# Block-sparse attention with a routed expert layer on one core: the chunk bounds computed with the queries as the stationary operand

## The chip, the cores and the metric

The kernel runs on one core of one Trainium2 chip. The metric is the device time of one execution in microseconds (us). A core has TensorE (PE, matrix products; it reads on-chip memory and writes only into PSUM, its result memory), VectorE (DVE) and ScalarE (ACT), which work on elements and read PSUM, GpSimd (POOL), and SyncE (SP), which here starts transfers. The engines run beside each other and wait for each other through semaphores.

A matrix product on PE has a stationary operand, which a weight load (PEld in the profile) puts into the array, and a moving operand, which is streamed through it; the result has one row per stationary column and one column per moving column. A turn is a transposition on PE: a product with the identity. In this kernel the scores and masks are bf16; keys, queries, bounds and values are fp32 on PE.

## The reference

Four batches, eight heads, 768 positions, head dimension 64. Keys come in 24 chunks of 32. For each query and chunk an upper bound of the scores is computed from the smallest and the largest key entries of the chunk; the six best chunks that are not in the future are kept, and attention runs on them alone. The heads' outputs then go through an expert layer with one of eight experts per token.

```python
k_min = np.min(k_chunks, axis=3)
k_max = np.max(k_chunks, axis=3)
ub = np.sum(np.maximum(q[:, :, :, None, :] * k_min[:, :, None, :, :],
                       q[:, :, :, None, :] * k_max[:, :, None, :, :]), axis=-1)
causal = pos[:, None] // chunk >= np.arange(nc)[None, :]
ub = np.where(causal, ub, -1000000000.0)
top_chunks = np.argsort(ub, axis=-1)[..., -top_k:]
scores = scale * np.matmul(q, k.transpose(0, 1, 3, 2))
# only keys of the chosen chunks, and not of the future; softmax; times v
...
expert_idx = np.argmax(x @ w_gate, axis=1)     # then relu(xe @ w1[e]) @ w2[e], times the gate
```

Since max(q a, q b) = (q (a + b) + |q| |a - b|) / 2, the bound is, up to a factor that does not matter for the order, a sum of two matrix products: q with (k_max + k_min), and |q| with (k_max - k_min).

## The kernel before

The 32 heads are worked on in 16 pairs; the two heads of a pair lie on partitions 0 to 63 and 64 to 127. Work is laid out in a fixed order on each engine: while pair `i` is in attention, the bounds and the selection of pair `n = i + 1` and the turns of keys and queries of pair `m = i + 2` are slipped in between. The order of the lines below is the order on each engine.

The first 128 queries have at most four chunks to see, so they need no selection. The bounds of the other 640 are computed with the chunk sums `ksd` stationary (2 heads x 32 columns) and 320 queries moving, twice for each half, the halves in different partitions of the result. So the bounds come out with chunks on partitions; ACT copies them to on-chip memory (`ub_a`), and three turns (`sel_mm`) bring the queries onto partitions, where DVE can rank along a row.

```python
c0s = (0, 128, 192)
...
        def ub():
            pu = ps_m.tile([128, 384], FP32, tag="m", name="pu")
            for w_, nm in ((0, "qT"), (1, "qA")):
                x_ = s[nm][:].rearrange("p a c -> p (a c)")
                for h in range(2):
                    nc.tensor.matmul(pu[64 * h:64 * h + 64, 0:320], lhsT=ksd[:, w_].rearrange("p a c -> p (a c)"),
                                     rhs=x_[:, ds(128 + 320 * h, 320)],
                                     start=(nm == "qT"), stop=(nm == "qA"), skip_group_check=True)
            s["pu"] = pu

        def ub_a():
            s["ubT"] = work.tile([128, 384], FP32, tag="ud", name="ubT")
            nc.scalar.activation(s["ubT"][:, 0:320], s["pu"][:, 0:320], AF.Copy)

        def sel_mm():
            pt = ps_m.tile([128, 3, 2, 2, 32], FP32, tag="m", name="pt")
            for t in range(3):
                nc.tensor.transpose(pt[:, t], s["ubT"][:, ds(c0s[t], 128)], ident_f[:])
            s["pt"] = pt

        def sel_v():
            ...                      # ubm = pt + cbias, 288 columns
            for t in range(3):
                for hf in range(2):
                    for hd in range(2):
                        nc.vector.max(out=top8[:, t, hf, hd], in_=ubm[:, t, hf, hd])
            ...                      # nsel = ubm < sixth best, 288 columns

        def mask():                  # six turns of nsel into pm
            ...
        def mask_a():                # ACT copies pm into qsb
            ...
```

One round of the loop, cut to what stands around these steps (groups 0 to 2 of four):

```python
                elif g == 0:
                    ...
                    av(i, 0)
                    av(i, 1)
                    ...
                    add(i, 1)
                    run(prep, n, "ub")
                    run(prep, n, "ub_a")
                    ...
                elif g == 1:
                    for u in (4, 5):
                        scores(i, u)
                        exps(i, u)
                    run(prep, n, "sel_mm")
                    if i > 0:
                        run(prep, m, "k_mm", 0)      # turns of the next but one keys
                        run(prep, m, "k_a", 0)
                    if router:
                        rank_mm()
                    run(prep, n, "sel_v")
                    ...
                    av(i, 2)
                    av(i, 3)
                    add(i, 3)
                    ...
                    scores(i, 6, True)
                    exps(i, 6)
                    ...
                elif g == 2:
                    ...
                    run(prep, n, "mask")
                    run(prep, n, "mask_a")
                    ...
                    av(i, 4)
                    av(i, 5)
```

`scores` writes into one of two PSUM buffers, `exps` is the exponential on ACT that frees it, `av` the product with the values, `add` the row sums on DVE. PSUM tiles of the tag "m" share three buffers in turn. The first pair has its own opening, in which `spin(n)` issues n products of ones, so that PE does not stand still.

Of the kernel before, what the change touches and what calls it, by code (L numbers as in the profile page):

```python
# [10 lines left out]
FP32 = mybir.dt.float32  # L11
BF16 = mybir.dt.bfloat16
# [12 lines left out]
def kernel(  # L25
# [10 lines left out]
    nc = tc.nc  # L36
# [22 lines left out]
    c0s = (0, 128, 192)  # L59
# [16 lines left out]
    cbias = const.tile([128, 3, 2, NCH], FP32)  # L76
# [18 lines left out]
    KSD = [buf.tile([128, 2, 2, 32], FP32, name=f"KSD{i}") for i in range(2)]  # L95
    bm = buf.tile([128, 2, NCH], BF16, name="bm")
    nsel = buf.tile([128, 3, 2, 2, 32], BF16, name="nsel")
# [5 lines left out]
    def consts_first():  # L103
# [18 lines left out]
        for t in range(3):  # L122
            nc.gpsimd.affine_select(out=cbias[:, t], in_=cbias[:, t], pattern=[[320, 2], [-CH, NCH]],
                                    compare_op=ALU.is_ge, fill=NEG, base=128 + c0s[t], channel_multiplier=1)
# [57 lines left out]
    def prep_steps(i):  # L182
# [23 lines left out]
        def kse():  # L206
            kt2 = work.tile([128, 2, NCH], FP32, tag="top8", name="kt2")
            nc.vector.tensor_tensor(kt2[:, 0], s["kmx"][:], s["kmn"][:], ALU.add)
            nc.vector.tensor_tensor(kt2[:, 1], s["kmx"][:], s["kmn"][:], ALU.subtract)
            nc.vector.tensor_tensor(ksd[:, :, :, 0:NCH], kt2[:].unsqueeze(2).to_broadcast([128, 2, 2, NCH]),  # L210
                                    bm[:].unsqueeze(1).to_broadcast([128, 2, 2, NCH]), ALU.mult)
# [21 lines left out]
        def ub():  # L233
            pu = ps_m.tile([128, 384], FP32, tag="m", name="pu")
            for w_, nm in ((0, "qT"), (1, "qA")):
                x_ = s[nm][:].rearrange("p a c -> p (a c)")
                for h in range(2):
                    nc.tensor.matmul(pu[64 * h:64 * h + 64, 0:320], lhsT=ksd[:, w_].rearrange("p a c -> p (a c)"),
                                     rhs=x_[:, ds(128 + 320 * h, 320)],
                                     start=(nm == "qT"), stop=(nm == "qA"), skip_group_check=True)  # L240
            s["pu"] = pu

        def ub_a():
            s["ubT"] = work.tile([128, 384], FP32, tag="ud", name="ubT")
            nc.scalar.activation(s["ubT"][:, 0:320], s["pu"][:, 0:320], AF.Copy)

        def sel_mm():
            pt = ps_m.tile([128, 3, 2, 2, 32], FP32, tag="m", name="pt")
            for t in range(3):
                nc.tensor.transpose(pt[:, t], s["ubT"][:, ds(c0s[t], 128)], ident_f[:])  # L250
            s["pt"] = pt

        def sel_v():
            pt = s["pt"]
            ubm = work.tile([128, 3, 2, 2, NCH], FP32, tag="ubm")
            nc.vector.tensor_tensor(ubm[:].rearrange("p n h d c -> p (n h) d c"),
                                    pt[:].rearrange("p n h d c -> p (n h) d c")[:, :, :, 0:NCH],
                                    cbias[:].rearrange("p n h c -> p (n h) c").unsqueeze(2)
                                    .to_broadcast([128, 6, 2, NCH]), ALU.add)
            top8 = work.tile([128, 3, 2, 2, 8], FP32, tag="top8")  # L260
            for t in range(3):
                for hf in range(2):
                    for hd in range(2):
                        nc.vector.max(out=top8[:, t, hf, hd], in_=ubm[:, t, hf, hd])
            u3 = ubm[:].rearrange("p a b c n -> p (a b c) n")
            t3 = top8[:].rearrange("p a b c n -> p (a b c) n")
            nc.vector.tensor_tensor(nsel[:].rearrange("p a b c n -> p (a b c) n")[:, :, 0:NCH], u3,
                                    t3[:, :, TOPK - 1:TOPK].to_broadcast([128, 12, NCH]), ALU.is_lt)

        def mask():  # L270
            pt = ps_m.tile([64, S], BF16, tag="m", name="pm")
            for hf in range(2):
                for t in range(3):
                    nc.tensor.transpose(pt[:, ds(128 + 320 * hf + c0s[t], 128)],  # L274
                                        nsel[:, t, hf].rearrange("p a n -> p (a n)"), ident_b[:])
            s["pm"] = pt

        def mask_a():
            for hd in range(2):
                nc.scalar.activation(qsb[64:64 + NCH, hd, 128:S], s["pm"][32 * hd:32 * hd + NCH, 128:S], AF.Copy)  # L280

        return dict(ub_a=ub_a, mask_a=mask_a, k_mm=k_mm, k_v=k_v, k_a=k_a, kse=kse, q_mm=q_mm, q_v=q_v, q_a=q_a, ub=ub,
                    sel_mm=sel_mm, sel_v=sel_v, mask=mask)


# [397 lines left out]
    def first_pair():  # L683
# [45 lines left out]
        consts_route(colf)  # L729
        prep[0]["ub"]()  # L730
        prep[0]["ub_a"]()
        kt(1)
        spin(8)
        prep[0]["sel_mm"]()
        spin(20)
        ubm = work.tile([128, 3, 2, 2, NCH], FP32, tag="ubm")
        top8 = work.tile([128, 3, 2, 2, 8], FP32, tag="top8")
# [3 lines left out]

        def select(hf):
            nc.vector.tensor_tensor(ubm[:, :, hf], s["pt"][:, :, hf, :, 0:NCH],
                                    cbias[:, :, hf].unsqueeze(2).to_broadcast([128, 3, 2, NCH]), ALU.add)
            for t in range(3):
                for hd in range(2):
                    nc.vector.max(out=top8[:, t, hf, hd], in_=ubm[:, t, hf, hd])
# [295 lines left out]
```

The softmax here doesn't subtract the row's maximum and nothing guards it: scores larger than these inputs give would overflow.

## Time and profile before

| What | Value |
|---|---|
| Time, median of three runs | 351.94 us (351.68 to 352.61) |
| Span of the profiled execution | 355.5 us |
| Mean granted TensorE clock | 0.988 of full |
| PE busy in 60 to 90 us | 29.79 of 30 us |
| DVE busy in 60 to 90 us | 27.95 of 30 us |
| ACT busy in 60 to 90 us | 25.32 of 30 us |
| Bounds on PE (L238), loads and products | 64 + 64 each for q and for its size |
| Copy of the bounds on ACT (L245) | 16 times, 446 ns (median) |
| Turns of the bounds on PE (L250) | 48 times, 273 ns (median) |
| Addition of the causal term on DVE (L256) | 15 times, 451 ns (median) |
| Maxima on DVE (L264) | 180 times, 168 ns (median) |
| Comparison on DVE (L267) | 15 times, 462 ns (median) |
| Turns of the mask on PE (L274) | 90 times, 219 ns (median) |

How to read it: the page of the profile gives first the busy time of each engine and its share of the span, then the span in 40 slices, each digit the busy share of that slice in tenths. Matmuls overlap[...]; so the distance from one start to the next says what a matmul costs, and its length does not. A weight load is listed apart (PEld) and usually runs beside the matmul before it. The rows below the first come from one profiled execution, the first from runs without a profile.

### The profile page before, as it was taken

Reading aid. Unit: us, or ns where it says so; the run is one execution under the profiler, and the core shown is the slowest. Engines: PE = TensorE matmul, PEld = TensorE weight load, DVE = VectorE, ACT = ScalarE, POOL = GpSimd, SP = SyncE. Lnnn points to the kernel's source line nnn. Section 1 sums busy time; section 2 is a strip of 40 time slices with the busy share of each in tenths; the row PEclk is TensorE's granted clock in tenths of the full one; section 3 lists DMA queues with packets and bytes.
Section 4 is the critical chain, followed back from the end, with each engine's and each line's share of the span. In section 5 each row is a group of like instructions: output and inputs, shape, how many; then the busy total and the mean of one; then the engine's idle time right before and its main releaser. Section 6 shows DMA issues by size and latency. Waiting matters only on the chain. (4 is left out here: it accounts for less than half of the span.)

```text
span 355.5 us, 7585 instructions
## 1 busy us (share of the span) xinstructions
PE 329.2 (93%) x2382; PEld 177.2 (50%) x2392; DVE 229.5 (65%) x776; ACT 230.4 (65%) x373; POOL 186.7 (53%) x300
## 2 busy tenths in 40 slices
PE   7889999999999999999999999977995899999992
PEld 7545656556555555555565555534441344444440
DVE  6688999999999999999999999941730000000000
ACT  2588788788796887886887977613323454544551
POOL 8515434536475437284355477583574556655323
PEclk9999999999999999999999999989998999999999
DMA  9998998899585897765979954969694999998962
GB/s 175 205 209 152 167 184 169 153 190 167 104 211 113 161 178 155 152 171 114 186 137 181 182 122 113 209 124 197 137 227 121 227 185 216 194 231 160 216 154 80
DMA packets 132071, 59.83 MB, mean 168 GB/s; under 512 B 122811, under 2 KB 122813, under 8 KB 132032
## 3 DMA queue, kind: packets, MB, share of 16 engines
q1 hardware_dynamic: 120640, 29.91, 43.5%
q0 software_dynamic: 11392, 29.42, 40.0%
q8 instruction: 21, 0.34, 0.4%
q14 instruction: 18, 0.15, 0.1%
HBM read 56.14 MB, written 10.51 MB: 188 GB/s over the span
## 5 line engine op out<-in xcount | busy, mean ns | idle before, releaser
L339 DVE TENSOR_TENSOR Pa<-Pa,Pr 128x768 f32<-128x768 f32 (+2 forms) x109 | 80.5, 742 | 4.3
L318 POOL TENSOR_SCALAR_AFFINE_SELECT Pr<-Pr 128x256 f32<-128x256 f32 x78 | 36.9, 492 | 77.9 <-ACT Pr L314 77.9
L314 ACT ACTIVATE Pr<-ps 128x768 f32<-128x768 f32 x79 | 62.6, 819 | 10.7 <-ACT KTE L203 4.3
L653 PE MATMUL py<-w_all,hT 128*128 x220 | 52.4, 379 | 3.0 <-issue 1.7
L298 PE MATMUL ps<-QSB,KTE 128*128 128x384 bf16 (+4 forms) x352 | 50.4, 283 | 1.5 <-ACT Pr L314 0.2
L661 POOL DMA_INDIRECT out_dram<-y,ti_all x28 | 28.0, 1001 | 37.2 <-ACT y L660 32.1
L298 PEld LDWEIGHTS <-KTE 128*128 128x128 bf16 (+1 forms) x352 | 26.5, 102 | 28.4 <-issue 22.0
L641 PE MATMUL ph<-w_all,KTE 128*128 x116 | 31.1, 413 | 6.3 <-ACT h__3986 L644 3.6
L653 PEld LDWEIGHTS <-hT 128*128 128x128 bf16 x224 | 21.8, 98 | 29.5 <-issue 1.8
L314 ACT ACTIVATE Pa<-ps 128x768 f32<-128x768 f32 x32 | 26.0, 812 | 14.0 <-PE ps L298 12.6
L660 ACT ACTIVATE y<-py,gt_all 128x512 f32<-128x512 f32 x27 | 18.6, 687 | 25.0 <-PE py L653 19.4
L203 ACT ACTIVATE KTE<-pk 64x384 bf16<-64x384 f32 x60 | 29.3, 488 | 7.1 <-DVE kmn L198 6.7
L493 POOL DMA_INDIRECT xs_dram<-xrow,sli x24 | 25.6, 1065 | 7.8 <-issue 5.7
L641 PE MATMUL ph<-w_all,QSB 128*128 x94 | 22.6, 379 | 1.6 <-DMA QSB<-xgqT 1.5
L641 PEld LDWEIGHTS <-KTE 128*128 128x128 bf16 x120 | 12.3, 104 | 23.0 <-issue 9.6
L280 ACT ACTIVATE QSB<-pm 24x640 bf16<-24x640 bf16 x30 | 20.8, 692 | 2.8 <-PE pm L274 2.1
L614 DVE TENSOR_TENSOR ti_all<-xgqA,inv_i 128x1 int32<-128x1 int32 x9 | 1.4, 160 | 30.7 <-DMA xgqA<-xs_dram,grow 26.1
L157 POOL DMA_DIRECT2D w_all<-in_moe_w_dram x32 | 21.1, 663 | 0.0
L197 DVE TENSOR_REDUCE kmx<-pk 128x12 f32<-128x384 f32 x32 | 17.6, 549 | 3.2 <-PE pk L192 3.0
L593 POOL DMA_INDIRECT xgqT<-xs_dram,grow x14 | 14.8, 1058 | 9.1 <-issue 6.2
L593 POOL DMA_INDIRECT xgqA<-xs_dram,grow x14 | 14.4, 1029 | 8.6 <-issue 4.7
L614 DVE TENSOR_TENSOR ti_all<-xgqT,inv_i 128x1 int32<-128x1 int32 x8 | 1.3, 159 | 25.7 <-DMA xgqT<-xs_dram,grow 20.9
(318 smaller groups left out, 635.9 us busy)
## 6 DMA issues: line engine op xcount, KB each, us to landing
w_all<-in_moe_w_dram POOLq DMA_DIRECT2D x32, 512.0 KB
out_dram<-y,ti_all POOLq DMA_INDIRECT x28
t__115<-in_k_dram SPq DMA_DIRECT2D x2, 192.0 KB
t__118<-in_q_dram SPq DMA_DIRECT2D x2, 192.0 KB
t__121<-in_v_dram SPq DMA_DIRECT2D x2, 192.0 KB
t__218<-in_k_dram SPq DMA_DIRECT2D x2, 192.0 KB
t__240<-in_q_dram SPq DMA_DIRECT2D x2, 192.0 KB
t__243<-in_v_dram SPq DMA_DIRECT2D x2, 192.0 KB
```

Source lines behind the costliest of these rows:

```text
L157: nc.gpsimd.dma_start(out=dst, in_=src.rearrange("(c p) f -> p c f" if n < 2 else "(p c) f -> p c f", p=128))
L203: nc.scalar.activation(kte[0:64, hd, ts(hf, 384)], pt[64 * hd:64 * hd + 64, :], AF.Copy, bias=0.0, scale=0.125)
L280: nc.scalar.activation(qsb[64:64 + NCH, hd, 128:S], s["pm"][32 * hd:32 * hd + NCH, 128:S], AF.Copy)
L298: nc.tensor.matmul(ps[ds(h * n, n), hd, ds(c0, w)], lhsT=kte[:, hd, ds(kb * 128 + h * n, n)], rhs=qsb[:, hd, ds(qb * 384 + 384 - w, w)], s ...
L314: nc.scalar.activation(P[:], ps[:, :, 0:384], AF.Exp)
L318: nc.gpsimd.affine_select(out=pd, in_=pd, pattern=[[0, 2], [1, 128]], compare_op=ALU.is_ge, fill=0.0, base=0, channel_multiplier=-1)
L339: nc.vector.tensor_tensor(acc[:, :, 384 - w:384], acc[:, :, 384 - w:384], P[:, :, ds(c0, w)], ALU.add)
L493: d = nc.gpsimd.indirect_dma_start(out=xs_dram[:], out_offset=bass.IndirectOffsetOnAxis(ap=sli[:, u:u + 1], axis=0), in_=bst[b][f"xrow{u % ...
L593: d = nc.gpsimd.indirect_dma_start(out=xg_bufs[j % XB].bitcast(I32), out_offset=None, in_=xs_dram[:], in_offset=bass.IndirectOffsetOnAxis( ...
L641: nc.tensor.matmul(ph[:, fh, :], lhsT=xT[:, c, :], rhs=w_all[:, ds(wo + (c * F + fh * 512), 512)], start=(c == 0), stop=(c == NDC - 1), sk ...
L653: nc.tensor.matmul(py[:], lhsT=hT[:, c, :], rhs=w_all[:, ds(wo + (W1W + c * DM), DM)], start=(c == 0), stop=(c == NFC - 1))
L661: d = nc.gpsimd.indirect_dma_start(out=out[:], out_offset=bass.IndirectOffsetOnAxis(ap=fs[j]["ti"], axis=0), in_=y[:], in_offset=None, bou ...
```

## The change

The roles in the bounds are swapped: for each of five blocks of 128 queries, the queries are stationary and the chunk sums (2 heads x 24 columns) move. So the bounds come out with queries on partitions at once; the ACT copy and the turns of the bounds fall away, and the selection reads the product directly. The six overlapping query pieces become five blocks, so DVE finds ten maxima instead of twelve, on 240 columns instead of 288, and the mask takes five turns instead of six. It is for taking a copy and a transposition out of the way from the bounds to the selection. The opening selects the first two blocks, then the other three, and makes its routing constants after the first selection instead of before; its warm-up products (8 and 20) become 28 in one go.

```diff
-    c0s = (0, 128, 192)
+    NQ = NT - 1
...
-    KSD = [buf.tile([128, 2, 2, 32], FP32, name=f"KSD{i}") for i in range(2)]
+    KSD = [buf.tile([128, 2, 2, NCH], FP32, name=f"KSD{i}") for i in range(2)]
...
         def ub():
-            pu = ps_m.tile([128, 384], FP32, tag="m", name="pu")
-            for w_, nm in ((0, "qT"), (1, "qA")):
-                x_ = s[nm][:].rearrange("p a c -> p (a c)")
-                for h in range(2):
-                    nc.tensor.matmul(pu[64 * h:64 * h + 64, 0:320], lhsT=ksd[:, w_].rearrange("p a c -> p (a c)"),
-                                     rhs=x_[:, ds(128 + 320 * h, 320)],
-                                     start=(nm == "qT"), stop=(nm == "qA"), skip_group_check=True)
-            s["pu"] = pu
-
-        def ub_a():
-            ...
-        def sel_mm():
-            ...
+            pt = ps_m.tile([128, NQ, 2, NCH], FP32, tag="m", name="pt")
+            for j in range(NQ):
+                for w_, nm in ((0, "qT"), (1, "qA")):
+                    nc.tensor.matmul(pt[:, j], lhsT=s[nm][:].rearrange("p a c -> p (a c)")[:, ds(128 * j + 128, 128)],
+                                     rhs=ksd[:, w_], start=(nm == "qT"), stop=(nm == "qA"), skip_group_check=True)
             s["pt"] = pt
...
+        def select(js):
+            n = len(js)
+            nc.vector.tensor_tensor(s["ubm"][:, js[0]:js[0] + n], s["pt"][:, js[0]:js[0] + n],
+                                    cbias[:, js[0]:js[0] + n].unsqueeze(2).to_broadcast([128, n, 2, NCH]), ALU.add)
+            for j in js:
+                for hd in range(2):
+                    nc.vector.max(out=s["top8"][:, j, hd], in_=s["ubm"][:, j, hd])
+            nc.vector.tensor_tensor(nsel[:, js[0]:js[0] + n, :, 0:NCH], s["ubm"][:, js[0]:js[0] + n],
+                                    s["top8"][:, js[0]:js[0] + n, :, TOPK - 1:TOPK].to_broadcast([128, n, 2, NCH]),
+                                    ALU.is_lt)
...
         def mask():
             pt = ps_m.tile([64, S], BF16, tag="m", name="pm")
-            for hf in range(2):
-                for t in range(3):
-                    nc.tensor.transpose(pt[:, ds(128 + 320 * hf + c0s[t], 128)],
-                                        nsel[:, t, hf].rearrange("p a n -> p (a n)"), ident_b[:])
+            for j in range(NQ):
+                nc.tensor.transpose(pt[:, ds(128 * j + 128, 128)], nsel[:, j].rearrange("p a n -> p (a n)"), ident_b[:])
...
         consts_last()
-        consts_route(colf)
         prep[0]["ub"]()
-        prep[0]["ub_a"]()
         kt(1)
-        spin(8)
-        prep[0]["sel_mm"]()
-        spin(20)
+        spin(28)
...
-        select(0)
+        prep[0]["sel_v"]((halves[0],))
+        consts_route(colf)
         mask_mm(0)
...
                     run(prep, n, "ub")
-                    run(prep, n, "ub_a")
...
-                    run(prep, n, "sel_mm")
```

## The prediction

> **What bounds the kernel now.** I read the page first: busy shares, then the forty slices.
>
> ```profile
> PE 329.2 (93%) x2382; PEld 177.2 (50%) x2392; DVE 229.5 (65%) x776; ACT 230.4 (65%) x373; POOL 186.7 (53%) x300
> ...
> PE   7889999999999999999999999977995899999992
> ...
> DVE  6688999999999999999999999941730000000000
> ACT  2588788788796887886887977613323454544551
> ```
>
> The first 26 slices (231 us of 355.5) are attention; the change touches nothing later. There PE and DVE both read 9 and ACT 6 to 8, so busy shares leave open which of PE and DVE sets the pace. A busy PE says little, as its matmuls overlap. So I read a stretch of one ordinary head pair in order of time, and compare starts, not durations. Columns: start in us, length, engine, line, operation, tiles, shape, count, and in brackets the idle time.
>
> ```profile
> 74.41 0.71 PE L238 MATMUL pu<-qT,KSD 128*64 128x320 f32 x4
> 74.95 0.71 PE L238 MATMUL pu<-qA,KSD 128*64 128x320 f32 x4
> 75.30 0.81 ACT L314 ACTIVATE Pr<-ps 128x768 f32<-128x768 f32 x1
> 75.59 1.05 PE L298 MATMUL ps<-QSB,KTE 128*128 128x384 bf16 x4
> 75.99 0.45 ACT L245 ACTIVATE ubT<-pu 128x320 f32<-128x320 f32 x1
> 76.50 0.55 PE L250 MATMUL pt<-ident_f,ubT 128*128 128x128 f32 x3
> 76.88 0.49 PE L192 MATMUL pk<-ident_f,t__1162 128*128 128x128 f32 x3
> ```
>
> PE goes from one group straight into the next. The bounds (L238) take 0.54 us per four passes, 1.08 us in all; about 0.1 us of changeover follows before the scores (75.59), the turn of the bounds (L250) begins right after them and takes 0.38 us. The ACT copy of the bounds between them (0.45 us) is hidden behind the score matmuls. The one real PE wait in this stretch is inside the scores: four of 0.16 us start at 75.59, so the third should start at 75.91, but its PSUM buffer is free only when the exponential that began at 75.30 ends (76.11). That is about 0.24 us.
>
> Then the waits of 20 to 232 us (who waited, for whom: total us, times, longest):
>
> ```profile
> PE pm L274 <- DVE nsel L267: 1.3, 3, 0.7
> PE po L331 <- DVE ot L346: 0.6, 2, 0.4
> PEld pt L250 <- ACT ubT L245: 2.8, 12, 0.2
> ```
>
> PE waits for DVE in only three pairs, those after a batch's routing, 1.9 us in all. Pairs repeat every 13.5 us (L238 starts at 60.9, 74.4, 87.9), and in most of them PE order is the pace. So a change to PE's work per pair goes almost fully into the time.
>
> **What the skill says.** "TensorE: Matmul & The Clock Gate", section "LDWEIGHTS (loading the stationary operand)": a load's time goes with the number of columns, at P / 1.2 ns, so 107 ns for 128. Section "Weight-path perf modes — Fast Weight Load (FWL) and DoubleRow" adds that the fast load needs 128 columns and a type other than fp32. "FP8 and Floating Point Precision", section "TensorE Precision Notes": a true fp32 product is four passes. "TensorEngine Tiling (Array Packing)", section "Key Properties": a change of tiling mode drains the engine. The trace of before agrees where it can be seen:
>
> ```profile
> L238 PEld LDWEIGHTS pu<-qT,KSD x64: 132/137/137, 9.6 to 213.9; 128*64 128x64 f32 x64
> L331 PE MATMUL po<-Pa,t__1016 x4: 486/512/537, 77.3 to 77.7; 128*64 128x384 f32 x4
> L362 PE MATMUL pu<-Pa,dcol x128: 486/498/510, 38.8 to 242.0; 128*32 128x384 f32 x128
> L274 PE MATMUL pm<-ident_b,nsel x90: 219/219/243, 26.9 to 220.0; 128*64 128x128 bf16 x90
> L250 PE MATMUL pt<-ident_f,ubT x48: 272/273/329, 11.4 to 216.3; 128*128 128x128 f32 x48
> ```
>
> (min/median/max ns.) The 16 pairs have 32 qT products of bounds and 64 loads: two loaded passes per product, each streaming both halves of the moving operand. The first product of a group shows in its maximum the load that nothing hid: 24 ns for 32 fp32 columns (L362), 51 for 64 (L331), 24 for 64 bf16 (L274), 56 for 128 fp32 columns in a turn (L250), which is one pass. So a two-pass fp32 load costs about 0.8 ns per column, and I estimate about 107 ns for 128 columns: the page's figure. No matmul of before loads 128 plain fp32 columns, so this is the least certain number here.
>
> **The change part by part, for one ordinary pair.**
>
> Removed from PE: 8 passes of bounds, 320 columns each, two column halves side by side: 1.08 us. Three turns: 0.38 us. One of six mask turns: in the same stretch five of them take 0.47 us and one alone 0.22, so (0.47 - 0.22)/4 = about 0.06 us.
>
> Added: ten products with 128 queries stationary and 48 columns moving, so 20 passes. Moving 48 fp32 columns takes 0.04 us (128 columns step every 0.11 us in L250), less than the load. The load of the next pass can run beside a pass, as it does between the turns, so a pass costs the load, 0.107 us by the estimate, with a little for the change from one to the next 0.109. The group costs about 0.10 us (changeover, now before the bounds instead of behind them) + 0.107 (first load, nothing hides it) + 19 x 0.109 + 0.04 = 2.31 us. The four score matmuls follow, 0.64 us, now without the wait of 0.24 us, because the exponential is long done. From the first bounds to the first turn of the next keys: before 76.88 - 74.41 = 2.47 us; after 2.31 + 0.64 = 2.95 us. That is +0.48, less 0.06 at the mask: **+0.43 us per ordinary pair**.
>
> ACT loses a copy of 0.45 us per pair (7 us in all), but this shortens no wait of an ordinary pair: ACT would instead sit idle until the later scores. The copy's PSUM buffer goes too, no gain where none was waited for.
>
> DVE: the addition and the comparison shrink from 288 to 240 columns (0.45 us for 288, 0.31 for 144 in the first pair: about 0.05 us less each); ten maxima replace twelve; twelve take 1.12 us there and one alone 0.17, so (1.12 - 0.17)/11 = 0.086 us each. Together **-0.28 us of DVE per pair**, which counts only where DVE is waited for.
>
> The sum. The loop computes bounds for 14 pairs.
> - Ten ordinary ones, routing pairs included: 10 x 0.43 = +4.3.
> - The first is still in the ramp; at 34 to 36 us its scores wait about 0.6 us in all for ACT, which hides most of the longer bounds: +0.1.
> - The three pairs in which PE waits for DVE: 3 x 0.43 - 1.9 = -0.6, since PE comes later and DVE is lighter.
> - The opening: the chain there is bounds, ACT copy, turns, first half of the selection, mask at 13.4 us. Now DVE can start on two blocks as soon as they are in PSUM, before the routing constants. 28 warm-up matmuls still stand ahead of the mask and PE's bounds are longer; I take -0.4. The first two pairs have waits of their own (a key load held PE 1.0 us at 26.4), so some may be lost.
>
> +4.3 + 0.1 - 0.6 - 0.4 = **+3.4 us: 355.3 us**, taken as 355.2. The expert stage shifts with the end of attention, unchanged.
>
> **Rivals.**
> 1. *128 plain fp32 columns load as fast as the turn's* (56 ns). For: the turn is fp32, 128 columns, in the full array; the columns that looked slow are all in column tiles. Against: 32 and 64 columns scale with their number and bf16 costs half. Then the bounds take 0.10 + 0.054 + 19 x 0.056 + 0.04 = 1.25 us; the scores keep their wait, the next turn starts at 2.07 instead of 2.47, and a pair gains 0.45 us: 10 x 0.45 + 3 x 0.28 (DVE sets those) + 0.8 at the start, about -6.2 us: 345.8 us. I give it 25%.
> 2. *Loads do not hide behind such short passes.* 0.107 + 0.04 per pass adds 0.76 us per pair: 10 x 1.19 + (3 x 1.19 - 1.9) + 0.9 - 0.4, about +14 us: 366 us. Against: between the turns the load starts right behind the start of the pass before and the step is 0.11 us. 10%.
> 3. *DVE or ACT is the real pace*, and removed work there pays: DVE reads 9 in the same slices. 0.28 us x 14 = -3.9 us, 348 us. Against: 1.9 us of PE waits on DVE in 212 us. As a whole account 5%; as part of the sum it is in.
>
> **Range and chances.** The mass lies at 353 to 358 us, a lump near 346, a thin tail to 366. Range 345.5 to 360.5. The 2% lines are 344.9 and 359.0: faster 0.10, same 0.75, slower 0.15.
>
> **What would show it.** In the changed profile: the 20 passes of an ordinary pair step by about 0.11 us and last 2.2 us (0.056 and 1.1 for rival 1, 0.15 and 3 for rival 2); weight loads of queries last about 190 ns, not 140; pair period near 13.9 us against 13.5; the score wait of 0.24 us gone; ACT at about 223 us busy; PE's waits on the selection mostly gone. I am wrong if the period falls, or if a wait I do not name, such as the attention products waiting for later exponentials, adds to the pair.

## The result, and the profile after

The changed kernel takes 361.65 us (median of four runs, 360.19 to 362.52). The kernel before takes 352.27 us beside it (median of four, 351.68 to 352.67). The ratio is 1.026, 95% interval 1.022 to 1.031: slower, and outside the predicted range of 345.5 to 360.5.

First the page of the changed kernel: busy time of each engine, and the rows of the forty slices that the prediction showed of before.

```profile
PE 336.9 (93%) x2510; PEld 200.1 (55%) x2520; DVE 229.3 (64%) x744; ACT 227.3 (63%) x357; POOL 187.4 (52%) x298
...
PE   8889999999999999999999999997997988999993
...
DVE  5688888898999988999988899971460000000000
ACT  2589778777777877878778777742343434444451
```

ACT's and DVE's digits in the attention stage are lower than before, PE's are nines as before. PE's busy time rose by 7.7 us and its loads' by 23 us. So the change did what it says to each engine; the page doesn't tell why a pair of heads grew by 0.92 us (below) where I had worked out 0.43.

Next the bounds line of the changed kernel (instruction, count, min/median/max in ns, first and last start in us, shape).

```profile
L237 PEld LDWEIGHTS pt<-KSD,qT x160: 186/192/193, 9.7 to 223.6; 128*128 128x128 f32 x160
L237 PE MATMUL pt<-KSD,qT x160: 275/275/311, 9.7 to 223.7; 128*128 128x48 f32 x160
```

The loads last 192 ns, as predicted (about 190), where the 64-column loads of before lasted 137. From one pass to the next there are 111 to 112 ns, for 109 predicted.

Now one ordinary pair in order of time, in the same columns as in the prediction (start, length, engine, line, operation, tiles, shape, count, idle time before it).

```profile
76.64 0.42 PE L237 MATMUL pt<-KSD,qT 128*128 128x48 f32 x2
...
78.91 0.81 PE L284 MATMUL ps<-QSB,KTE 128*128 128x384 bf16 x4
...
79.49 1.51 ACT L300 ACTIVATE Pr<-ps 128x768 f32<-128x768 f32 x2 [1.25 <-issue]
79.56 0.49 PE L191 MATMUL pk<-ident_f,t__1141 128*128 128x128 f32 x3
...
82.83 2.25 DVE L325 TENSOR_TENSOR Pa<-Pa,Pr 128x768 f32<-128x768 f32 x2
...
83.25 2.10 POOL L304 TENSOR_SCALAR_AFFINE_SELECT Pr<-Pr 128x256 f32<-128x256 f32 x2
...
85.32 0.85 POOL L392 TENSOR_TENSOR lg<-lg,lgt 128x96 f32<-128x96 f32 x2
...
86.20 0.42 DVE L381 TENSOR_TENSOR lgt<-pl,rec 128x96 f32<-128x96 f32 x2 [0.83 <-POOL lg L392]
...
86.72 0.97 PE L218 MATMUL pq<-ident_f,t__1144 128*128 128x128 f32 x6 [0.31 <-PE pk L191]
...
87.37 0.77 POOL L304 TENSOR_SCALAR_AFFINE_SELECT Pr<-Pr 128x256 f32<-128x256 f32 x2 [0.29 <-ACT Pr L300]
```

The head of it is what I had predicted: the bounds fill 76.64 to 78.91, the scores follow without a wait (79.56 - 78.91 = 0.65 us for four), then the turns of the next keys. The new thing is eight microseconds further on, in the turns of the queries (L218): 0.31 us of idle time ahead of them, put down to the turns of keys. The turns of keys are only the last thing that PE itself did. What the query turns need is a PSUM buffer: they take the one that held the turned logits (L371), the third last to be taken from three in turn, and DVE reads that one until the second of its two products L381 ends, at 86.20 + 0.42 = 86.62. The turns start 0.10 us later. DVE in its turn waited 0.83 us for GpSimd (the bracket on L381): the logits have one buffer, and GpSimd must first have added up the logits that the pair before had left there (L392). And GpSimd's order is fixed: its additions stand behind a row of work that could begin only when the exponential of the sixth unit had ended, at 79.49 + 1.51 = 81.00 us. From 81.08 on it has no gap: one causal cut (L304) of the sixth unit, two casts, the issue of a weight load (82.50), and at 83.25 the two cuts of the seventh unit.

The same stretch of the kernel before:

```profile
80.12 1.48 POOL L318 TENSOR_SCALAR_AFFINE_SELECT Pr<-Pr 128x256 f32<-128x256 f32 x2 [0.21 <-ACT Pr L314]
...
80.39 2.02 DVE L339 TENSOR_TENSOR Pa<-Pa,Pr 128x768 f32<-128x768 f32 x2
...
81.57 1.54 POOL L406 TENSOR_TENSOR lg<-lg,lgt 128x96 f32<-128x96 f32 x2
...
83.14 0.42 DVE L395 TENSOR_TENSOR lgt<-pl,rec 128x96 f32<-128x96 f32 x2 [0.40 <-POOL lg L406]
...
83.67 0.97 PE L219 MATMUL pq<-ident_f,t__1165 128*128 128x128 f32 x6
```

The chain is there too: cuts, additions, logits to 83.56, query turns at 83.67, again 0.11 us later. PE just had work until then. And GpSimd still waited 0.21 us (the first bracket) for the exponential of the seventh unit, whose scores come in PE's own order. In the changed kernel this wait is gone: work taken from PE lets the chain end sooner only until GpSimd has no gap left. In the list of waits of before over 20 to 232 us, DVE's wait for GpSimd is already there (who waited, for whom: total us, times, longest us):

```profile
DVE lgt L395 <- POOL lg L406: 2.4, 6, 0.4
```

and after it has doubled, and PE's own wait has joined it (20 to 238 us of the changed kernel):

```profile
DVE lgt L381 <- POOL lg L392: 5.0, 6, 0.8
PEld pq L218 <- PE pk L191: 3.9, 8, 0.5
PE pq L218 <- PE pk L191: 2.1, 7, 0.3
```

The waits that the prediction showed of before, of PE for the selection and of the turn's load for the ACT copy, are no longer among the larger ones. Cut into three legs by starts, the ordinary pair reads:

| Leg, us | Before | After | Difference | Predicted |
|---|---|---|---|---|
| First bounds to first scores | 75.59 - 74.41 = 1.18 | 78.91 - 76.64 = 2.27 | +1.09 | +1.03 |
| First scores to query turns | 83.67 - 75.59 = 8.08 | 86.72 - 78.91 = 7.81 | -0.27 | -0.68 |
| Query turns to next bounds | 87.91 - 83.67 = 4.24 | 91.06 - 86.72 = 4.34 | +0.10 | +0.10 |
| Period | 13.50 | 14.42 | +0.92 | +0.45 |

The predicted column takes the prediction's 2.31 us apart into 0.10 of changeover and 2.21, and its savings behind the scores (three turns 0.38, one mask turn 0.06, the score wait 0.24) together; its +0.45 differs from the recorded +0.43 by rounding. Only the middle leg is off by much.

Over the whole stage: the last bounds start at 221.7 us instead of 213.9 (+7.8), and the first product of the expert stage at 245.67 instead of 236.43 (+9.2), close to the difference of the medians (9.4). The spans of the two profiled executions differ by only 5.2 us because the profiled one of before was itself 5 us above its median: its expert stage took 119 us, that of after 115.

### The profile page after: what moved, and what is told of

Read it like the earlier page. It is cut to its first block, busy times and chain, and to the rows that moved or that the text cites. A ratio compares the mean times of both kernels' runs of the same rounds, so it can differ in the third digit from the quotient of the medians.

```text
span 360.7 us, 7770 instructions
## 1 busy us (share of the span) xinstructions
PE 336.9 (93%) x2510; PEld 200.1 (55%) x2520; DVE 229.3 (64%) x744; ACT 227.3 (63%) x357; POOL 187.4 (52%) x298
## 5 line engine op out<-in xcount | busy, mean ns | idle before, releaser
L304 POOL TENSOR_SCALAR_AFFINE_SELECT Pr<-Pr 128x256 f32<-128x256 f32 x78 | 42.5, 564 | 90.1 <-ACT Pr L300 90.0
L325 DVE TENSOR_TENSOR Pa<-Pa,Pr 128x768 f32<-128x768 f32 (+2 forms) x109 | 82.9, 763 | 4.3
L284 PE MATMUL ps<-QSB,KTE 128*128 128x384 bf16 (+4 forms) x352 | 47.7, 283 | 0.0
L284 PEld LDWEIGHTS <-KTE 128*128 128x128 bf16 (+1 forms) x352 | 27.8, 105 | 17.0 <-issue 9.8
L300 ACT ACTIVATE Pa<-ps 128x768 f32<-128x768 f32 x32 | 25.9, 811 | 13.5 <-PE ps L284 13.2
L627 PE MATMUL ph<-w_all,KTE 128*128 x116 | 29.4, 396 | 4.1 <-DMA KTE<-xgqT 3.1
L237 PE MATMUL pt<-KSD,qT 128*128 128x48 f32 x160 | 31.5, 279 | 1.1 <-DVE qT L701 1.1
L237 PE MATMUL pt<-KSD,qA 128*128 128x48 f32 x160 | 31.0, 275 | 0.0
L237 PEld LDWEIGHTS pt<-KSD,qT 128*128 128x128 f32 x160 | 24.2, 191 | 3.9 <-issue 2.4
L237 PEld LDWEIGHTS pt<-KSD,qA 128*128 128x128 f32 x160 | 24.3, 192 | 0.0
```

Of the source, the lines that this page charges most:

```text
L237: nc.tensor.matmul(pt[:, j], lhsT=s[nm][:].rearrange("p a c -> p (a c)")[:, ds(128 * j + 128, 128)], rhs=ksd[:, w_], start=(nm == "qT"), s ...
L284: nc.tensor.matmul(ps[ds(h * n, n), hd, ds(c0, w)], lhsT=kte[:, hd, ds(kb * 128 + h * n, n)], rhs=qsb[:, hd, ds(qb * 384 + 384 - w, w)], s ...
L300: nc.scalar.activation(P[:], ps[:, :, 0:384], AF.Exp)
L304: nc.gpsimd.affine_select(out=pd, in_=pd, pattern=[[0, 2], [1, 128]], compare_op=ALU.is_ge, fill=0.0, base=0, channel_multiplier=-1)
L325: nc.vector.tensor_tensor(acc[:, :, 384 - w:384], acc[:, :, 384 - w:384], P[:, :, ds(c0, w)], ALU.add)
L627: nc.tensor.matmul(ph[:, fh, :], lhsT=xT[:, c, :], rhs=w_all[:, ds(wo + (c * F + fh * 512), 512)], start=(c == 0), stop=(c == NDC - 1), sk ...
```

## The experiments

The comparisons below are each with the kernel before in runs made together with them. Its median differed from set to set (352.0, 358.2, 352.7 or 358.5 us), so ratios, not times, compare experiments of different sets. "Period" is the distance from the bounds of one ordinary pair to those of the next; 13.5 us before, 14.4 after.

**Theory.** Behind the scores of the fifth and sixth unit a chain ACT, GpSimd, DVE, PSUM buffer takes some 7.7 us even when PE is ready sooner; before, PE's own work in that leg was a little longer (8.0 us). The turns and waits taken from PE there are hidden by it, and only the longer bounds show. **Rivals:** the loads cost more than I estimated; the later exponentials alone make the wait; the transfers or DVE set the pace.

### The loads doubled

Each product of the changed kernel is split by head, so that 40 passes with as many loads replace 20, each moving half as many columns.

```diff
-                    nc.tensor.matmul(pt[:, j], lhsT=...ds(128 * j + 128, 128)], rhs=ksd[:, w_], ...)
+                    for hd in range(2):
+                        nc.tensor.matmul(pt[:, j, hd], lhsT=...ds(128 * j + 128, 128)], rhs=ksd[:, w_, hd], ...)
```

> Each bounds product of the changed kernel is split by head into two of 24 moving columns, so the moved columns stay the same and the loads of 128 query columns double from 20 to 40 per pair. If a pass costs its weight load (0.112 us in the changed kernel's trace), the bounds take 4.5 us per pair instead of 2.25, the pair period rises from 14.4 to about 16.7 us, and with 15 pairs the time goes from 361.7 to about 395 us. If the bounds cost by the columns that are streamed, nothing changes: about 362 us.

Measured: 427.8 us (427.2 to 428.4, two runs) against 352.0, ratio 1.217 (1.209 to 1.226). The step between passes stayed at 112 ns with half the columns, so the load alone sets it; 40 passes took 4.4 to 4.5 us where they ran clean. That is 2.2 us more per pair, some 31 us over fourteen pairs, and settles what a load costs. The rest of the 66 us above the changed kernel, 35 us, needs another cause. The slices of the granted clock and the bounds line of this run:

```profile
PEclk9688696988969897896989879896989999999999
```

```profile
L238 PEld LDWEIGHTS pt<-KSD,qT x320: 186/192/338, 8.3 to 288.2; 128*128 128x128 f32 x160
L238 PE MATMUL pt<-KSD,qT x320: 269/269/389, 8.3 to 288.3; 128*128 128x24 f32 x160
```

The mean granted clock fell to 0.894 (0.992 in the changed kernel), in stretches with steps of 213 ns, and the longest loads are 338 ns. In the trace the clock stands at 0.50 for 90 us in all, 5 us in the changed kernel; half of the 85 us more, an estimate of the PE time that this costs, is 42 us and enough for the rest. DVE waited 35 us for the bounds in all. In this run, where the product of the other head is begun before the second half of a sum is added, the sums come out wrong and other chunks are chosen. The next run was to take that away.

> As the doubled loads, but both products of one head directly after each other, so no other product starts in between. The load theory expects 40 passes of 0.112 us again, 4.5 us per pair. If starting a product in neighbouring columns is what spoiled the sums of the doubled loads, they are right here; if narrow products of 24 columns spoil them, they are not.

In this variant both halves of one head come before the other head's:

```diff
-                for w_, nm in ((0, "qT"), (1, "qA")):
-                    for hd in range(2):
+                for hd in range(2):
+                    for w_, nm in ((0, "qT"), (1, "qA")):
```

Measured: 433.7 us in one run, where the kernel before took 358.2; clock 0.895, passes again 112 ns; and the sums are whole. So the 0.9 clock belongs to the many short loaded passes and not to wrong selections. I did not find out what in them lowers it.

### Half tiles

The 128 queries as two tiles of 64 columns, side by side; the same bounds in the same places.

```diff
-                    nc.tensor.matmul(pt[:, j], lhsT=...ds(128 * j + 128, 128)], rhs=ksd[:, w_], ...)
+                    for h in range(2):
+                        nc.tensor.matmul(pt[64 * h:64 * h + 64, j],
+                                         lhsT=...ds(128 * j + 128 + 64 * h, 64)], rhs=ksd[:, w_], ...)
```

> The queries stay stationary, but 64 at a time, in two halves of the array that write partitions 0 to 63 and 64 to 127 of the same result. If a load costs by the columns of its own half (51 ns for 64 in the trace of before) and the halves load side by side, 20 steps of about 0.056 us make the bounds 1.1 us per pair, the exponentials are not late any more, the pair period is about 13.1 us against 14.4 and before's 13.5, and the time is about 346 us, below both kernels. If both halves share one way in, the 128 columns per step cost 0.112 us as before: about 361 us.

Measured: 351.6 us (348.4 to 357.0, 20 runs), ratio 0.997 (0.994 to 1.000). The bounds line and, from PE's waits over the whole run, the longest:

```profile
L238 PEld LDWEIGHTS pt<-KSD,qT x320: 133/138/138, 9.6 to 215.0; 128*64 128x64 f32 x160
```

```profile
PE pk L191 <- DMA t__403<-in_k_dram: 3.9, 1, 3.9
```

The two halves load beside each other: a pair of passes steps by 58 ns, and from the first pass to the scores there are 1.25 us instead of 2.27 (1.18 before). That takes away nearly all of the cost which the change had brought. The ordinary periods are 12.99 to 13.45, on average 13.3 against 13.5. So with the load's cost gone the change is a gain of 0.2 us per pair, not the 0.6 by which PE's work is shorter (0.68 behind the scores, less 0.07 ahead of them); PE still waits for the PSUM buffer in every other pair, and DVE is busy 28.96 of the 30 us from 60 to 90. The gain of the pairs was spent in one place: PE waited 3.9 us for the third load of keys, 1.0 us before. In this profile the granted clock then stood at 0.50 for 6.8 us, so that the period with the wait took 18.3 us instead of 12.8.

> A second profile of the half tiles: bounds again 1.1 us per pair. If the wait of 4 us for a key load in the ramp was chance, it is absent or elsewhere and the last bounds start near 210 us instead of 214; if it belongs to the kernel, it is there again.

This run is the half tiles once more, unchanged: 357.0 us in one run, where the kernel before took 358.2. Its profile has the wait for the third load of keys too (3.7 us, from 23.0 us), so that wait isn't chance. The clock stayed at full behind it, and the period with the wait took 15.4 us. The ordinary periods are 12.99 to 13.47.

### Two buffers for the logits

In the changed kernel, the logits get a second buffer, so that DVE need not wait for GpSimd's additions.

```diff
-            lgt = work.tile([128, 6, 2, 2, E], FP32, tag="lgt")
+            lgt = work.tile([128, 6, 2, 2, E], FP32, tag="lgt", bufs=2)
...
```

Two other tiles that share this buffer, in the opening and in the routing, get the same `bufs=2`.

> The changed kernel with two buffers for the logits that DVE writes and GpSimd adds up. Theory: in the changed kernel the later exponentials make GpSimd late, DVE waits for it with the logits (0.8 us in an ordinary pair), and so the query turns on PE wait about 0.43 us for a PSUM buffer. With two logit buffers this wait falls away: pair period about 14.0 us instead of 14.4, time about 357 us, and the wait of the query turns gone. Rival: the rise beyond the bounds themselves comes from elsewhere on PE; then the period stays at 14.4 and the time at about 361.5 us.

Measured: 359.2 us (356.7 to 361.0, four runs) against 352.0, ratio 1.020 (1.013 to 1.027). The period falls from 14.42 to 13.88, and the wait at the query turns is gone: from start to start it adds up to 0.58 us over fourteen pairs, 3.56 in the changed kernel. Two lines from its waits of 20 to 240 us:

```profile
PE pk L191 <- DMA t__393<-in_k_dram: 2.7, 1, 2.7
...
PE pq L218 <- PE pk L191: 0.2, 1, 0.2
```

DVE's wait for GpSimd no longer appears in that list at all. This confirms the link of the chain that was read from one coincidence in time, and 13.88 is within 0.05 us of the period that the prediction's sum gives (13.50 + 0.43). But the seven ordinary pairs should have given 7 x 0.54 = 3.8 us, and the time fell by 2.4 us in ratio terms (1.0263 to 1.0196), with intervals that overlap: the period and the wait show the effect, the time alone does not. The first line shows one place where it went: this profile has 2.7 us of waiting for the third load of keys (PE's gap there is 0.4 us in the changed kernel), and 1.4 us for two later ones.

Half tiles and two buffers together (both diffs above):

> Half tiles and two logit buffers together. If the query turns' wait, still 0.44 us in every other ordinary pair of the half tiles, comes from the single logit buffer, it goes, and the ordinary period is an even 13.0 us, with DVE (28.96 of 30 us busy) as the next limit: about 349 us. If DVE is already the pace, the period stays at 13.2 us on average and the time at about 351.5 us.

Measured: 357.5 us (354.5 to 365.4, 12 runs) against 358.2, ratio 1.000 (0.995 to 1.004); periods 12.94 to 13.39; 4.3 us of waiting for the third load of keys. With the short bounds the second buffer brings 0.05 to 0.07 us in six of the seven ordinary pairs, and the query turns still wait 0.37 us in every other one (0.43 without it): there the logit buffer is no longer the main thing that they wait for. DVE, busy 28.96 of 30 us here too, is the likely pace; I did not lighten it to see.

### The bounds split around the scores

The first three blocks of the bounds stay ahead of the scores, the last two come behind them, so that the exponentials start 0.9 us earlier and PE has the same work.

```diff
-                    run(prep, n, "ub")
+                    run(prep, n, "ub", range(0, 3))
...
                     for u in (4, 5):
                         scores(i, u)
                         exps(i, u)
+                    run(prep, n, "ub", range(3, NQ))
```

> The changed kernel with the last two of its five bounds blocks computed after the scores of units 4 and 5 instead of before them, so PE's work is the same and these exponentials start about 0.9 us earlier. If the late exponentials are what makes GpSimd, then DVE, then the query turns late, the wait of the turns (0.43 us per pair) goes: period about 14.0 us, about 357 us. If lateness of the exponentials plays no part, about 361.5 us.

Measured: 355.4 us (352.3 to 357.2, 15 runs) against 352.0, ratio 1.009 (1.005 to 1.012). The period is 13.96, and the wait at the query turns 0.43 us over all pairs. No pass, load or turn differs from the changed kernel, so the order alone costs 1.8% in ratio. What is left, +0.46 us per pair and +3.0 us in the ratio, is the sum of the prediction (+0.43 and +3.4): with the chain covered, PE's order is the pace again. This run and the one with two logit buffers leave DVE's work and the transfers as they are, so neither of these sets the pace of the changed kernel.

### The kernel before with later exponentials

The product with q is done three times in the kernel before, each time from the start, so the exponentials come 1.07 us later and nothing behind them changes.

```diff
-            for w_, nm in ((0, "qT"), (1, "qA")):
+            for w_, nm in ((0, "qT"), (0, "qT"), (0, "qT"), (1, "qA")):
```

> The kernel before with its first bounds product (q with the sums) done three times over, each time from the start, so the values stay as they are. PE gets 8 more side-by-side passes, 1.07 us per pair, in the same place, with the old small loads; the exponentials of units 4 and 5 come as late as in the changed kernel. Of the 1.07 us the score wait of 0.24 us is absorbed: +0.84 us. If late exponentials cost by themselves (GpSimd, then DVE, then the query turns), another 0.3 to 0.45 us: pair period 14.7 to 14.8 us, time about 364 to 366 us, and a new wait of the query turns in its trace. If the wait in the changed kernel has to do with its own buffers or its selection instead, period 14.35 us, about 361 us, no such wait.

Measured: 368.7 us (368.0 to 370.8, four runs) against 358.2, ratio 1.031 (1.024 to 1.038); period 14.37; at the query turns 0.47 us over all pairs, so no wait. The rival's period (14.35) came out, and no wait, as it said; the ratio lies between the two sides (361 us is 1.026 of 352, 364 to 366 us are 1.034 to 1.040). Late exponentials alone don't make the wait, because they delay PE as much as the chain: the bounds stand ahead of both. That narrowed the theory to the leg from the scores on. Here are the four kernels in that leg, us from the start of the scores of the fifth unit in one ordinary pair, read from starts and ends in the traces; the last but one row is PE's own steps up to the query turns, without the wait:

| | Before | After | Before, late | Bounds split |
|---|---|---|---|---|
| GpSimd's cuts end | 6.00 | 6.43 | 6.49 | 6.87 |
| GpSimd's additions end | 7.52 | 7.25 | 7.31 | 7.69 |
| DVE's logits end | 7.98 | 7.71 | 7.77 | 8.14 |
| PE could start the query turns | 8.04 | 7.33 | 7.79 | 8.18 |
| Query turns start | 8.08 | 7.81 | 7.87 | 8.24 |

In all four the turns start 0.10 us behind the logits. In the column After, PE was ready 0.48 us ahead of its turns; in the others it was less than 0.1 us, so PE and the chain run level there. PE lost 8.04 - 7.33 = 0.71 us of work in this leg, and the chain let 0.27 of it through. (GpSimd's wait for the seventh unit, ahead of its cuts, is 0.21, 0, 0 and 0.75 us in the four.)

### The expert weights' loads moved

In the half tiles the two 512 KB weight loads that the opening starts just ahead of the third key load are moved into the first passes of the pair loop.

```diff
-    npiece = [1, 2, 2, 2, 2, 1, ...]
+    npiece = [2, 3, 2, 2, 2, 1, ...]
...
         mask_in(1)
-        for _ in range(2):
-            load_w(next(wnext))
```

> The half tiles again, with the loads of the expert weights that stand in the opening, just ahead of the third key load, moved behind it into the pair loop. Theory (the third key load is late because two 512 KB weight loads share the transfer engines with it): the wait of about 4 us for the third key load falls to 0 to 1 us, the third pair's bounds start at about 34 us instead of 38, the ordinary periods stay at about 13.2, and the whole comes to about 347 to 348, a ratio of 0.985 to 0.99. Rival (the transfers as a whole are the limit of this stretch): the wait stays or moves to a later key or query load, and the time is that of the half tiles, a ratio of 0.997.

> Control for e9: the kernel before with the same move of the weight loads and nothing else. Theory: its wait of 1.0 us for the third key load goes, its periods stay at 13.5, and it gains 0.5 to 1 us, a ratio of 0.997 to 0.999. Rival (the place of the weight loads is worth the same to both kernels): a gain of 3 us or more here too, a ratio of 0.99 or less.

In the second of these expectations "e9" is the run of the first.

Measured: the half tiles take 348.2 us (345.7 to 352.5, six runs) against 352.7, ratio 0.986 (0.982 to 0.991), and the third pair's bounds start at 30.7 us instead of 38.1. This is the best version of the study, 4.5 us under the kernel before. The kernel before with the same move takes 360.1 us (358.1 to 360.7, six runs), ratio 1.021 (1.017 to 1.025), which neither side expected. Its third key load came at once and its second period fell by 1.0 us, as expected; but then it waited for the fourth (PE's waits, then the issues of the fourth load):

```profile
PE pk L192 <- DMA t__569<-in_k_dram: 4.9, 1, 4.9
```

```profile
L178 SPq DMA_DIRECT2D t__569<-in_k_dram x2: 385/614/842, 28.9 to 29.3; - x2
```

That period took 21.7 us instead of 13.8: behind the wait of 4.9 us the granted clock stood at 0.50 for 6.8 us. The moved weight loads started at 27.7 and 28.2, the key load 0.7 us behind the second, at 28.9, and the turns could start only at 40.6. In the half tiles the weight loads started at 24.9 and 25.4, the key load 1.4 us behind, and PE waited only 1.3 us. The listings of the transfers from 10 to 50 us (KB each, us from issue to landing; of the two transfers of this load each trace has the landing of the first alone) show the third load of keys beside the two weight loads in the half tiles, and without them in the half tiles with moved loads and in the kernel before with moved loads, in this order:

```profile
t__403<-in_k_dram SPq DMA_DIRECT2D x2, 192.0 KB, 10.4
```

```profile
t__401<-in_k_dram SPq DMA_DIRECT2D x2, 192.0 KB, 5.3
```

```profile
t__400<-in_k_dram SPq DMA_DIRECT2D x2, 192.0 KB, 3.0
```

The Trainium skill, "DMA: Bandwidth & Descriptors", section "Issuing engines are not separate DMA queues", says that transfers of all issuing engines share the same 16 DMA engines and interleave; here the first transfer of a key load took 10.4 us beside the two weight loads and 5.3 or 3.0 us without them.

So the move was put where no pass has two weight loads just ahead of a key load, at least up to the fourth:

```diff
-    npiece = [1, 2, 2, 2, 2, 1, ...]
+    npiece = [1, 2, 3, 3, 2, 1, ...]
```

> The half tiles with the two weight loads of the opening moved to the third and fourth passes of the pair loop, so that no two weight loads start just ahead of the fourth key load, as they do when the first two passes take them. Theory (a key load that starts within about a microsecond of two weight loads lands 10 to 12 us later, one that starts beside one or none lands after 3 to 7 us): no key load is waited for by more than 0.5 us in this stretch, the second and third pairs take 11.6 and about 13.4 us, and the whole comes to 346 to 348.5, a ratio of 0.981 to 0.988. Rival (the loads as a whole are the limit): the wait moves to a later key or query load of about 2 us or more, and the ratio is 0.99 or above.

> The kernel before with the weight loads moved as in e11, the control for it. Theory: the 5 to 8 us that the fourth key load cost in the run with the loads in the first two passes go, the third key load is not waited for either (1.0 us in the kernel before), and the time is 0.5 to 1.5 us under the kernel before, a ratio of 0.995 to 0.999; the half tiles then keep a lead of 1.0 to 1.5% from their shorter bounds, not from the transfers. Rival (the gain of the half tiles with late weights is the transfers' alone): this one gains as much, a ratio of 0.988 or less.

In these two, "e11" is the first run, and "the run with the loads in the first two passes" is the one just reported.

Measured: the half tiles 358.7 us (352.9 to 362.7, 22 runs) against 358.5, ratio 0.994 (0.991 to 0.997); the kernel before 358.7 us (356.7 to 365.6, 22 runs), ratio 1.000 (0.997 to 1.002). The ratio leaves out runs more than 1.5% above the fastest of their kernel (12 of the 22 of the half tiles, the profiled one among them), while over all runs the medians are equal: 0.994 is a weak sign of a gain. Against my theory, in favour of its rival: no key load is waited for up to 49 us, and then, where a pass starts two weight loads at 49.4 and 50.0 us, the next one is, by 3.0 us, though it starts 3.7 us behind them; that pair takes 17.8 us.

In the kernel before, no key load is waited for any more, but two later periods are 0.5 and 0.4 us longer. The wait there is at the query turns, not for a load. The second of the two is a further trial of the chain, though it was not meant as one: the pass that starts two weight loads from 65.3 us keeps GpSimd at that for 1.29 us instead of 0.57, between its first cut and the two others. GpSimd's cuts end 7.1 us behind the scores of the fifth unit (6.0 before), DVE's logits 8.36 (7.98), and 0.10 us behind these the query turns start, for which PE had been ready for 0.43 us. In PE's waits of this run this is:

```profile
PE pq L219 <- PE pk L192: 0.5, 2, 0.3
```

So the kernel before has the wait too when the chain alone is made longer, with its own bounds and buffers.

For the half tiles, where the two weight loads fall goes with 0.986 or 0.994, for the kernel before with 1.000 or 1.021. The lead of the half tiles over the kernel before is 0.3% in the old placement (its interval reaches 1.000), 0.6% in the spread one by the ratios, none by the medians of all runs, and 3.4% in the first two passes, most of which is what the kernel before loses there.

## Why the prediction was wrong

*The passes and loads: right.* 0.112 us per pass for 0.109, the whole group with its changeover 2.37 us for 2.31, the loads 192 ns for 190. The estimate of 107 ns for a load of 128 columns stands, and rivals 1 (56 ns) and 2 (0.147 us) are out.

*The score wait: right.* Four scores take 0.65 us, 0.64 predicted. *DVE: right.* The three groups of the selection take 0.40 + 0.95 + 0.41 = 1.76 us for 0.45 + 1.12 + 0.47 = 2.04, the -0.28 of the prediction; PE's waits for the selection are gone from the top of the list. *ACT: right, though not by its number.* It is 227.3 us busy for 223, but no group of its instructions grew: their lengths add up to 243.8 us before and 235.5 after, and 7.2 of the difference are the copies. The busy time counts records that overlap once, and there is less overlap after (8.2 us for 13.4).

*"A change to PE's work per pair goes almost fully into the time": this step failed.* It was read from a stretch in which PE goes from one group into the next without a gap. That a PE has no gaps says only that nothing else is slower now, and not by how much. Behind the scores the chain through ACT, GpSimd and DVE ran level with PE, within 0.1 us, in the kernel before. I took 0.68 us from PE in that leg and counted it in full; 0.27 came through, and for the rest PE waits for a PSUM buffer ahead of the query turns (3.56 us over fourteen pairs). The term of the sum that was mis-sized is -0.68, which measured -0.27, and the pair went from +0.43 to +0.92. The run with the bounds split shows the same sum coming out right once the chain is covered; the run with two logit buffers shows the chain's link, and the kernel before with spread weight loads shows the wait without the change.

*The copy of the bounds "shortens no wait of an ordinary pair: ACT would instead sit idle until the later scores": true, and passed over too quickly.* ACT did sit idle for 1.25 us ahead of the exponentials, and these then stand at the head of the chain. The sign that I named for being wrong, a wait that I do not name such as one behind later exponentials, was the right kind. It is not the attention products that wait, but the query turns.

*The total.* Ten pairs at +0.43 were to give 4.3 us. The seven ordinary ones gave 7.2 (0.9 each, 1.4 and 1.2 in two of them, one with 0.7 us of waiting for a key load), the three with routing 1.0: 3.9 more. The opening with the first three periods gave -0.1 for -0.3, two of the three behind a routing pair -0.3 for -0.4. The last pair, with the stretch up to the expert stage, gave +1.4 for -0.2. Of that, 0.4 lies ahead of the end of the last exponential, and 1.0 between it and the first expert product, a stretch that varies from 4.4 to 6.5 us over these runs, also in kernels with the bounds of before; I don't put it down to the change. Sum: +9.2 for +3.4, where the medians differ by 9.4.

## What to carry to other kernels

An engine without gaps can still be one of two that run level. Before counting work taken from it as time saved, follow every other chain from the same starting point to the next place where they meet (here from the scores over GpSimd and the logits to one PSUM buffer) and note how much room each has: what is taken beyond the smallest room is not saved. With a narrow moving side the load of the stationary side can be the price of a product (here 112 ns a pass with 48 moving columns and with 24), and two half-width tiles beside each other paid it at once (58 ns); and when an opening becomes faster, look which large transfers now stand just ahead of a small urgent one.

## What the runs showed of the hardware that I had not expected

- *GpSimd beside DVE.* Two causal cuts took 2.10 us at 83.25, while DVE ran additions of two on-chip operands (82.83, 2.25 us), and 0.77 us at 87.37, when it ran none. In the kernel before, where the cuts began 0.27 us ahead of such additions, they took 1.48 us, and GpSimd's own additions beside these 1.54 us, 0.85 where DVE's had ended. The Trainium skill, "SBUF — State Buffer", section "Who interferes with whom", says that a DVE instruction with two on-chip inputs contends with a GpSimd instruction that reads on-chip memory; the numbers agree, though the spans of GpSimd are rough. This is a part of the chain's length, and no run took it away.
- *The clock under short loaded passes.* With 40 passes per pair instead of 20, PE without gaps was granted 0.894 of its clock in the mean, with stretches at 0.50 and steps of 213 ns instead of 112. The cause stays open.
- *The clock behind a long wait.* Behind waits of PE for a key load of 3.9, 4.3 and 4.9 us the granted clock stood at 0.50 for 6.8 us, behind one of 3.0 us for 3.4; behind others of 3.7 and 2.7 us it stayed at full. So a late load can cost more than its wait.
- *Transfers.* The first 192 KB of a key load landed after 3.0 or 5.3 us without two weight loads of 512 KB beside it and after 10.4 us with them; how far behind them it starts (0.7 or 1.4 us) went with 4.9 or 1.3 us of waiting, though one that started 3.7 us behind them was still waited for by 3.0 us. How the distance acts was not tried by itself.
